# Weight conversion paced over the first expert, five pieces of it in the attention stage; token gather ahead of later weight loads; load queue in the attention plan

## The chip, the cores and the metric

The kernel runs on one core of a Trainium2 chip. The metric is the device time of one execution in microseconds (us). The engines are named as the profile names them: PE is TensorE (PEld its weight loads), DVE VectorE, ACT ScalarE, POOL GpSimd, SP SyncE, which here only issues DMAs.

## The reference

Three stages follow one another: a gated linear attention, a mixture of 8 experts with 384 tokens each, and a gated feed-forward layer that is the same for all tokens.

```python
def reference(**kwargs):
    attn_out = _attn_ref(q, k, v, a_re, a_im)      # (4, 8, 768, 48)
    x = attn_out.transpose(0, 2, 1, 3).reshape(B * S, H * D)   # 3072 x 384
    x = _moe_ref(x, w_gate, w1, w2)     # 8 experts, 384 -> 1024 -> 384
    return _moe2_ref(x, w_a, w_b, w_out)

def _attn_ref(...):          # complex decay a_re + i a_im, state 48 x 48 per head
    for t in range(S):
        new_re = ar * S_re - ai * S_im
        new_im = ar * S_im + ai * S_re
        S_re, S_im = new_re + outer(k[t], v[t]), new_im
        y[t] = q[t] @ S_re

def _moe_ref(x, w_gate, w1, w2):
    order = np.argsort(-(x @ w_gate).flatten())    # greedy: best logit first,
    # a token to one expert, an expert takes at most 384
    h = np.maximum(x[mask] @ w1[e], 0.0)
    out[mask] = h @ w2[e]

def _moe2_ref(x, w_a, w_b, w_out):      # 384 -> 1536 -> 384, float64 weights
    return ((x @ w_a) * (x @ w_b)) @ w_out
```

The weights of the last layer arrive in 64-bit floats and are handed to the kernel as pairs of 32-bit words.

## The kernel before, in words

**Attention.** The sequence is cut into 6 chunks of 128 steps; a pass i works on one chunk of two batches, 12 passes in all (`NB`). Each pass turns the decays into logarithms and angles (`gates`), sums them along the chunk on PE (`sums`), makes the turned q and k (`turned`), and for chunks after the first brings the state forward (`factor`, on 16 partitions). `unit` does the matmuls of one batch: transposes, scores, outer products, output. Nothing of this is issued directly: every step is a task of a `Plan`, with an engine, a planned duration, what it reads and writes, and a due time (`PERIOD` per pass). `Plan.order` walks through the tasks on a model of the engines and issues, each time, the ready task of lowest rank; the rank comes from the due time times `STRETCH`, the length of the chain behind the task, and an offset per kind of task from the table `EARLIER`; `SWITCH` is added where ACT would have to load another function table. SP's DMAs are tasks too (line 329 loads the decays, 332 and 334 q, k and v, 448 and 363 single rows for `factor`, 517 and 518 a swap of two halves of the state).

**Routing.** `route` finds each expert's threshold by five rounds of counting on DVE and PE, `lists` turns the choice into row numbers `idx`, `gather` fetches the 384 rows from `x_dram` with three indirect DMAs (tile `xg`, line 1216), transposes them on PE and splits them into two fp32r halves, `xh` and `xl`. The splits of weights and activations into such halves are helpers on lines 1153 (ACT) and 1154 (DVE). `w1_load` (line 1188) and `w2_load` (line 1202) fetch expert weights by indirect DMA, all from POOL. `R.keep` lets PE do matmuls whose result nobody reads.

**Experts.** `ffn(ph)` runs one expert: stage 1 (w1 and w2, 8 steps f with two `yield`s each, 144 matmuls of 128x384 on lines 1249 to 1251), then stage 2 (the last layer for the same tokens, 12 steps f with three `yield`s, 324 matmuls, lines 1301 and 1249 to 1251). The second-stage weights stay on chip in four `groups` of 9 pieces, 36 in all.

**Conversion.** `Glu.convert` makes these 36 pieces from the 64-bit words: a DMA of 384 KB (`load`, SP line 726), three steps on ACT (735, 741, 752) and three on DVE (745 `sign`, 749 `join`, 756 `low`). It is a generator with three `yield`s a piece, so 108 steps.

**What goes beside what.** During routing `beside` takes one conversion step for each routing step. In the first expert the loop at the end takes `CONV_RATE` = 4 conversion steps per `yield` of `ffn(0)`, and `SIDE_RATE` = 0.9 steps of the next expert's routing and loading (`later`), which may not load before the conversion has ended (`S["conv"]`):

```python
for n, _ in enumerate(ffn(ph)):
    due += CONV_RATE if ph == 0 else 0
    while due >= 1:
        due -= 1
        step(more, CONV_AFTER)
    k += SIDE_RATE if n < 16 else SIDE_RATE2
    while k >= 1:
        k -= 1
        step(it)
```

DVE takes its instructions in the order in which the code is written there (`manual_schedule`); the order of the other engines' instructions in this part is made by the compiler layer.

Of the kernel before, what the change touches and what calls it, by code (L numbers as in the profile page):

```python
# [10 lines left out]
F32 = mybir.dt.float32  # L11
# [23 lines left out]
SWITCH = 61.0  # L35
# [5 lines left out]
PIECES = 0  # L41
EARLIER = {'Acc': -2, 'Ae': 99, 'Aea': 39, 'Afw': 11, 'Ag': -75, 'Aln': -20, 'Apb': -27, 'AqkT': 9, 'Arec': 15, 'As2': -5, 'Asf': -11, 'Ath': 58, 'Axo': 8, 'AyT': -36, 'G-': -59, 'GW': -21, 'Gconsts': 2, 'Gmasks': 51, 'Gzeros': -28, 'PF': -33, 'PHH': -2, 'PLL': -39, 'PO': 68, 'PS': -40, 'PTT': 90, 'PX': 59, 'PY': 126, 'Sends': 69, 'Sfw': 67, 'Sim': -99, 'Sqk': 72, 'Sraw': -57, 'Sre': 2, 'Ssw': -147, 'Sv': -41, 'V-': 19, 'VAb': -10, 'VS': 99, 'Ve': 29, 'Vearly': -29, 'Veb': 55, 'Vft': -4, 'Vg': -28, 'Vlg': 5, 'Vn4': -38, 'Vnat': -69, 'Vr': 33, 'Vrho': 89, 'Vrt0': -55, 'Vrt1': -13, 'Vsetup': -54, 'Vxs': -152}
STRETCH = 3.699071
LONG = ("LL", "HH")
ENGINES = "PVASG"
SLOW = 1.03
SINGLE = 1
PATIENCE = 7
ENOUGH = 21.5
# [7 lines left out]
class Plan:  # L57
# [8 lines left out]
    def add(self, eng, dur, fn, reads=(), writes=(), due=0.0, take=None, drop=None, table=None, land=0.0):  # L66
        t = dict(n=len(self.tasks), eng=eng, dur=dur * SLOW if eng == "P" else dur, fn=fn, due=due, take=take, drop=drop, table=table, land=land,
# [21 lines left out]
    def order(self):  # L89
# [12 lines left out]
        free = dict.fromkeys(ENGINES, 0.0)  # L102
        for t in T:
            if not left[t["n"]]:
                waiting[t["eng"]].append(t["n"])
# [14 lines left out]
        while any(waiting.values()):  # L120
# [71 lines left out]
def attention(tc, q, k, v, a_re, a_im, wg, x_dram, consts, L, guard, router, glu, late):  # L192
# [8 lines left out]
    with ExitStack() as st:  # L201
# [26 lines left out]
        for nm, x in (("one", 1.0), ("shift", LIFT), ("tiny", LN(2.0e-6)), ("quarter", HALF_PI)):  # L228
            bias[nm] = cst.tile([128, 1], F32, name="b_" + nm)
            V.memset(bias[nm], x)  # L230
# [86 lines left out]
        def gates(i, due):  # L317
# [5 lines left out]
            load, land = (2.3, 2.2) if i < 2 else (0.6, 3.8)  # L323
            for us in parts(i):
# [3 lines left out]
                for nm, t, src in (("re", ld_re, a_re), ("im", ld_im, a_im)):  # L328
                    plan.add("S", took(load, us), lambda t=t, src=src, r=r, at=at, d2=d2: SP.dma_start(t[j][:, r], flat(src, at, d2)),
                             writes=[(nm, j, u) for u in us], due=due - 20 - 40 * (i < 2), land=land)  # L330
            for x, src in ((0, q), (1, k)):
                plan.add("S", load, lambda x=x, src=src: SP.dma_start(ld_qk[j][:, x], flat(src, base, dims)),
                         writes=[("qk", j, x)], due=due - 10, land=land)
            plan.add("S", load, lambda: SP.dma_start(vb[j].rearrange("p u h d -> p (u h) d")[:, :, 0:D], flat(v, base, dims)),
                     writes=[("v", j)], due=due - 4, land=land)
# [79 lines left out]
        def turned(i, due):  # L415
# [37 lines left out]
            if c < NCK - 1:  # L453
                w = (i + 2) % 4
                row(fw[w][:, 0], ("fw", w, 0), s2, both(ks2), 127)
                row(fw[w][:, 1], ("fw", w, 1), sn, both(ksn), 127)
            if c:
                w = i % 4
                row(fw[w][:, 2], ("fw", w, 2), s2, both(ks2), 0)
                row(fw[w][:, 3], ("fw", w, 3), sn, both(ksn), 0)  # L460

        def factor(i, due):
# [8 lines left out]
            plan.add("A", 0.22, lambda: A.activation(f[:, 4], f[:, 7], AF.Sin, bias=bias["quarter"][0:16]),  # L471
                     [kf[7]], [kf[4]], table="T", **a)
            plan.add("A", 0.22, lambda: A.activation(f[:, 5], f[:, 7], AF.Sin), [kf[7]], [kf[5]], table="T", **a)
            sh = [2 * H, 2, 2, D]

            def one():
                V.tensor_scalar(f[:, 0:3:2], f[:, 0:3:2], -1.0, 1.0, op0=OP.mult, op1=OP.add)
                V.tensor_tensor(w[:, 0:4].rearrange("p (a b) d -> p a b d", a=2), f[:, None, 0:2].to_broadcast(sh),
                                f[:, 2:4, None].to_broadcast(sh), op=OP.mult)
                V.tensor_tensor(w[:, 4], w[:, 0], w[:, 3], op=OP.add)  # L480
                V.tensor_tensor(w[:, 5], w[:, 1], w[:, 2], op=OP.subtract)
            plan.add("V", 0.92, one, kf[0:4], [kw, kf[0], kf[2]], **a)

            def two():
                V.tensor_tensor(w[:, 0:4].rearrange("p (a b) d -> p a b d", a=2), w[:, None, 4:6].to_broadcast(sh),
                                f[:, 4:6, None].to_broadcast(sh), op=OP.mult)
                V.tensor_tensor(w[:, 6], w[:, 0], w[:, 3], op=OP.subtract)
                V.tensor_tensor(w[:, 7], w[:, 1], w[:, 2], op=OP.add)
            plan.add("V", 0.66, two, [kw] + kf[4:6], [kw], **a)

            def three():
                V.scalar_tensor_tensor(w[:, 4], ends[:, i - 2, 0], math.exp(-2 * LIFT), ends[:, i, 1], op0=OP.mult, op1=OP.mult)
                V.tensor_tensor(w[:, 5], w[:, 4], f[:, 6], op=OP.mult)
                sh2 = [2 * H, 2, D]
                V.tensor_tensor(w[:, 8:10], w[:, 6, None].to_broadcast(sh2), w[:, 5, None].to_broadcast(sh2), op=OP.mult)
                V.tensor_tensor(w[:, 10], w[:, 7], w[:, 5], op=OP.mult)
# [1162 lines left out]
```

## Time and profile before

| | |
|---|---|
| median of 3 runs | 1066.19 us (1063.6 to 1066.37) |
| profiled execution, own time | 1064.48 us |
| its span, first to last instruction | 1062.9 us |
| mean granted TensorE clock | 0.975 of full |
| PE busy in the span | 994.7 us (94%) |
| DVE busy | 640.8 us (60%) |
| ACT busy | 501.8 us (47%) |

The shares are means over stages with different limits. Attention runs to about 288 us, routing to 329, the first expert from 329.1 to 436.6, and the seven others from there to the end. A busy PE is a modelled quantity, since matmuls overlap. [...]

### The profile page before, as it was taken

The page shows a single profiled execution, that of the slowest core. Times are in us where ns is not written, and L with a number is a line of the kernel's source. Part 1 is how long each engine was busy: PE and PEld are TensorE (multiplying, and loading weights), DVE is VectorE, ACT ScalarE, POOL GpSimd, SP SyncE. Part 2 cuts the span into 40 slices and gives each one's busy share as a digit, 9 for nine tenths or more (in the row PEclk, how much of TensorE's full clock was granted, in tenths as well). Part 3 has the DMA queues.
Part 4 walks back from the last instruction along what each step waited for, and adds up shares of the span by engine and source line. Part 5 has one row for each costly group of instructions (what it writes and reads, how often), then busy time and mean ns, then how long its engine had stood idle before and what let it go on. Part 6 is the DMA issues. An engine that isn't in the chain of part 4 may idle for free. (4 is left out here: it accounts for less than half of the span.)

```text
span 1062.9 us, 17395 instructions
## 1 busy us (share of the span) xinstructions
PE 994.7 (94%) x6660; PEld 901.2 (85%) x6660; DVE 640.8 (60%) x1596; ACT 501.8 (47%) x906; POOL 164.6 (15%) x217
## 2 busy tenths in 40 slices
PE   3899999999987699999999999999999999999994
PEld 1588787888746599999989999999999999999994
DVE  4689888998677987555366355455536644333321
ACT  6799898887426773332332332243233234233221
POOL 6000000000021003203112120320311213102001
PEclk9999999999968789999999999999999999999998
DMA  9866777344145644102112110310211212201000
GB/s 170 129 120 124 121 130 135 74 89 111 42 140 166 177 143 127 53 8 96 33 38 79 42 45 1 105 52 8 90 35 42 69 47 78 76 15 45 1 2 26
DMA packets 146764, 81.90 MB, mean 77 GB/s; under 512 B 130416, under 2 KB 132336, under 8 KB 146672
## 3 DMA queue, kind: packets, MB, share of 16 engines
q1 hardware_dynamic: 134448, 41.36, 20.4%
q0 software_dynamic: 12224, 39.34, 11.6%
q8 instruction: 54, 0.88, 0.3%
q14 instruction: 38, 0.31, 0.1%
HBM read 68.04 MB, written 9.44 MB: 73 GB/s over the span
## 5 line engine op out<-in xcount | busy, mean ns | idle before, releaser
L1301 PE MATMUL mm<-yh,glu 128*128 128x384 f32 x1152 | 241.7, 344 | 0.0
L1301 PEld LDWEIGHTS mm<-yh,glu 128*128 128x128 f32 x1152 | 201.5, 189 | 2.1 <-ACT yh L1153 0.4
L1335 DVE TENSOR_TENSOR g<-mm,a_s 128x384 f32<-128x384 f32 x96 | 53.4, 556 | 154.7 <-PE mm L1301 130.4
L1301 PE MATMUL mm<-yl,glu 128*128 128x384 f32 x576 | 133.2, 338 | 0.0
L1153 ACT ACTIVATE gh<-g 128x384 fp32r<-128x384 f32 x96 | 50.4, 525 | 163.5 <-DVE g L1335 163.5
L1330 ACT ACTIVATE a_s<-mm 128x384 f32<-128x384 f32 x96 | 47.1, 491 | 151.1 <-PE mm L1301 142.7
L1301 PEld LDWEIGHTS mm<-yl,glu 128*128 128x128 f32 x576 | 103.4, 187 | 0.0
L1249 PE MATMUL acc<-glu,gh 128*128 128x384 f32 x288 | 98.4, 342 | 0.0
L1250 PE MATMUL acc<-glu,gh 128*128 128x384 f32 x288 | 96.9, 336 | 0.0
L1251 PE MATMUL acc<-glu,gl 128*128 128x384 f32 x288 | 96.7, 337 | 0.1
L1202 POOL DMA_INDIRECT raw<-moe_w_in,i x64 | 64.2, 1004 | 171.0 <-DVE w2l L1154 121.5
L1154 DVE TENSOR_TENSOR gl<-g,gh 128x384 fp32r<-128x384 f32 x96 | 53.6, 558 | 40.8 <-ACT gh L1153 39.9
L1250 PE MATMUL acc<-hl,w2h 128*128 128x384 f32 x192 | 67.0, 349 | 5.2 <-DVE hl L1276 5.2
L1249 PE MATMUL mm<-xh,w1h 128*128 128x384 f32 x192 | 67.4, 352 | 0.4 <-ACT w1h L1153 0.3
L1251 PE MATMUL acc<-hh,w2l 128*128 128x384 f32 x192 | 66.1, 344 | 0.0
L1251 PE MATMUL mm<-xh,w1l 128*128 128x384 f32 x192 | 65.1, 339 | 1.1 <-DVE w1l L1154 1.1
L1249 PE MATMUL acc<-hh,w2h 128*128 128x384 f32 x192 | 65.8, 353 | 0.2 <-ACT hh L1275 0.2
L1250 PE MATMUL mm<-xl,w1h 128*128 128x384 f32 x192 | 65.0, 339 | 0.0
L1188 POOL DMA_INDIRECT raw<-moe_w_in,i x24 | 24.2, 1008 | 253.1 <-DVE left L1062 172.5
L1153 ACT ACTIVATE w1h<-raw 128x384 fp32r<-128x384 f32 x64 | 32.7, 521 | 54.1 <-PE mm L1250 51.6
L552 PE MATMUL bank<-qkT 96*128 96x128 f32 x384 | 54.1, 286 | 3.7 <-ACT qkT L543 3.4
L1154 DVE TENSOR_TENSOR w1l<-raw,w1h 128x384 fp32r<-128x384 f32 x64 | 34.9, 552 | 36.3 <-ACT w1h L1153 29.8
(277 smaller groups left out, 2007.7 us busy)
## 6 DMA issues: line engine op xcount, KB each, us to landing
stage<-moe_w_a_in SPq DMA_DIRECT2D x13, 384.0 KB, 3.2
vb<-v_in SPq DMA_DIRECT2D x12, 384.0 KB, 5.0
ld_qk<-q_in SPq DMA_DIRECT2D x12, 384.0 KB, 4.3
ld_qk<-k_in SPq DMA_DIRECT2D x12, 384.0 KB, 5.8
x_rows<-xo POOLq DMA_DIRECT2D x24, 192.0 KB, 2.4
stage<-moe_w_b_in SPq DMA_DIRECT2D x12, 384.0 KB, 3.2
stage<-moe_w_out_in SPq DMA_DIRECT2D x12, 384.0 KB, 3.5
ld_im<-a_im_in SPq DMA_DIRECT2D x11, 384.0 KB, 5.9
```

The source lines that it names most:

```text
L552: PE.matmul(p[:, x], qt[0:96, 4 * h4 + x, 1], qt[0:96, 4 * h4 + x, 0], start=True, stop=True)
L1153: a = A.activation(hi, src, AF.Copy)
L1154: return a, V.tensor_tensor(lo_, src, hi, op=OP.subtract)
L1188: G.indirect_dma_start(out=raw[:, j], out_offset=None, in_=w1r, in_offset=bass.IndirectOffsetOnAxis(ap=i1[:, j:j + 1], axis=0))
L1202: G.indirect_dma_start(out=raw, out_offset=None, in_=w2r, in_offset=bass.IndirectOffsetOnAxis(ap=i2[:, f:f + 1], axis=0))
L1249: PE.matmul(p, lh, rh, start=first, stop=False)
L1250: PE.matmul(p, lh, rl, start=False, stop=False)
L1251: PE.matmul(p, ll, rh, start=False, stop=last)
L1301: PE.matmul(p, a[:, j, c], b[:, j], start=(n == 0), stop=(n == 8))
L1330: A.activation(a_s, pa, AF.Copy)
L1335: V.tensor_tensor(g, pb, a_s, op=OP.mult)
```

## The change

Six things change. (1) Five pieces are converted inside attention, as tasks of the plan (`PIECES` 0 to 5). (2) The rest is paced: 1.2 steps per `yield` in stage 1 of the first expert, 2.2 in stage 2, and `Glu.need` takes the steps at once that a group is about to need; the steps of the next expert's routing go at 0.5 and then 1.15, and no longer wait for the conversion's end. (3) The first expert's w1 is fetched in two halves, and POOL, now in written order too, issues the gather behind the first half and one w2 load, and the other half behind the gather. (4) The dummy matmuls before the gather go from 24 to 36. (5) The plan counts the time that a DMA holds the load queue (`wire`), and its constants and the table `EARLIER`, one line of offsets for some fifty kinds, have new values. (6) `factor` takes the difference of angles first, so that one row r is sent by DMA in place of the rows of s2 and sn, and 10 small DVE instructions stand for 12.

```diff
-SWITCH = 61.0
+SWITCH = 186
...
-PIECES = 0
+PIECES = 5
...
-STRETCH = 3.699071
+STRETCH = 3.100414
...
-ENOUGH = 21.5
+ENOUGH = 21.0
...
+            sent = end
+            if e == "S":
+                sent = max(end, wire)
+                wire = sent + t["wire"]
             for u in users[n]:
                 left[u] -= 1
-                ready_at[u] = max(ready_at[u], end + t["land"] + (HOP[e] if T[u]["eng"] != e else 0.06))
+                ready_at[u] = max(ready_at[u], sent + t["land"] + (HOP[e] if T[u]["eng"] != e else 0.06))
...
-                row(fw[w][:, 0], ("fw", w, 0), s2, both(ks2), 127)
-                row(fw[w][:, 1], ("fw", w, 1), sn, both(ksn), 127)
+                row(fw[w][:, 0], ("fw", w, 0), r, both(kr), 127)
...
+            def angle():
+
+                V.scalar_tensor_tensor(f[:, 0], f[:, 7], 0.5 / PI, f[:, 0], op0=OP.mult, op1=OP.add)
+                V.tensor_tensor(f[:, 0], f[:, 0], f[:, 1], op=OP.subtract)
...
-WARM = 24
+WARM = 36
...
-CONV_RATE = 4
+SIDE_RATE0 = 0.5
+SIDE_RATE1 = 1.15
+CONV_RATE = 1.2
+CONV_RATE2 = 2.2
...
+    def need(self, pieces):
+
+        while self.at < min(pieces, 36) and next(self.more, 0) is None:
+            pass
...
+            else:
+                w1_half(0)
+
+        def w1_half(x):
             for j in range(3):
-                G.indirect_dma_start(out=raw[:, j], out_offset=None, in_=w1r,
-                                     in_offset=bass.IndirectOffsetOnAxis(ap=i1[:, j:j + 1], axis=0))
+                G.indirect_dma_start(out=S["raw1", 0][:, j, F1 // 2 * x:F1 // 2 * (x + 1)], out_offset=None, in_=w1s,
+                                     in_offset=bass.IndirectOffsetOnAxis(ap=S["i1", 0][:, 3 * x + j:3 * x + j + 1], axis=0))
...
             if ph == 0:
-                for f in (1, 2):
-                    w2_load(ph, f)
+                w2_load(ph, 1)
+                w1_half(1)
+                w2_load(ph, 2)
...
             for f in range(12):
+                glu.need(9 * (f // 3) + 3)
...
+                glu.need(9 * (f // 3) + 6)
...
-        with tc.manual_schedule(engines={V.engine}):
-            more = rest()
+        with tc.manual_schedule(engines={V.engine, G.engine}):
+            more = glu.more = rest()
...
-                    while S["moe"] < n - 1 or not S["conv"]:
+                    while S["moe"] < n - 1:
...
-            due = 0
+            due = glu.steps
             for n, _ in enumerate(ffn(ph)):
-                due += CONV_RATE if ph == 0 else 0
-                while due >= 1:
-                    due -= 1
+                due += CONV_RATE if n < 16 else CONV_RATE2
+                while glu.steps < min(due, 108):
                     step(more, CONV_AFTER)
-                k += SIDE_RATE if n < 16 else SIDE_RATE2
+                if ph == 0:
+                    k += SIDE_RATE0 if n < 16 else SIDE_RATE1
+                else:
+                    k += SIDE_RATE if n < 16 else SIDE_RATE2
```

**DVE in stage 1 of the first expert,** from the fifth `hl` (the second half of an activated block, which PE needs for the next step) to the sixth. `stage` and `glu` are conversion steps, `w1l` and `w2l` weight splits, the small names the next expert's routing. Before:

```order
L1276 SCALAR_TENSOR_TENSOR hl<-mm,hh 128x384
L756 TENSOR_TENSOR glu_2652<-stage,glu_2652 128x384
L749 SCALAR_TENSOR_TENSOR stage<-stage 128x384
L1154 TENSOR_TENSOR w1l<-raw_2949,w1h 128x384
L745 SCALAR_TENSOR_TENSOR stage<-stage 128x384
L1005 TENSOR_REDUCE cn<-misc 32x8
L756 TENSOR_TENSOR glu_2652<-stage,glu_2652 128x384
L749 SCALAR_TENSOR_TENSOR stage<-stage 128x384
L1007 TENSOR_TENSOR c_3323<-cn,rem 32x8
L1154 TENSOR_TENSOR w2l<-raw_3278,w2h 128x384
L745 SCALAR_TENSOR_TENSOR stage<-stage 128x384
L1276 SCALAR_TENSOR_TENSOR hl<-mm,hh 128x384
```

Changed, between the same two:

```order
L1307 SCALAR_TENSOR_TENSOR hl<-mm,hh 128x384
L1023 TENSOR_TENSOR c_3206<-cn,rem 32x8
L1170 TENSOR_TENSOR w1l<-raw_2944,w1h 128x384
L758 SCALAR_TENSOR_TENSOR stage<-stage 128x384
L1170 TENSOR_TENSOR w2l<-raw_3243,w2h 128x384
L754 SCALAR_TENSOR_TENSOR stage<-stage 128x384
L1029 TENSOR_REDUCE n<-misc 128x1
L1170 TENSOR_TENSOR w1l<-raw_2944,w1h 128x384
L765 TENSOR_TENSOR glu_2645<-stage,glu_2645 128x384
L1030 SCALAR_TENSOR_TENSOR lo<-n,steps,lo 128x1
L1307 SCALAR_TENSOR_TENSOR hl<-mm,hh 128x384
```

Six conversion steps stood between these two `hl`, now three. Over the stage, from the first `hl` to the first `yl`, 47 stood there before and 18 now; ahead of the first `hl` there were 25 and are 41; behind the first `yl` 36 and now 49.

**ACT just before the first expert,** where `raw_2953` and `raw_2948` are its w2 block 0, `raw_3028` and `raw_3035` its block 1, and `xh` the gathered rows behind their transposes. Before:

```order
L1153 ACTIVATE w1h<-raw_2949 128x384 x2
L1153 ACTIVATE w2h<-raw_2953 128x384
L1153 ACTIVATE w2h<-raw_3028 128x384
L741 ACTIVATE stage<-stage 128x384
L752 ACTIVATE glu_2247<-stage 128x384
L1153 ACTIVATE xh<-mm 128x3x128
```

Changed:

```order
L1169 ACTIVATE w2h<-raw_2948 128x384
L744 ACTIVATE stage<-stage 128x384
L750 ACTIVATE stage<-stage 128x384
L761 ACTIVATE glu_2645<-stage 128x384
L744 ACTIVATE stage<-stage 128x384
L750 ACTIVATE stage<-stage 128x384
L761 ACTIVATE glu_2645<-stage 128x384
L1169 ACTIVATE w2h<-raw_3035 128x384
L1169 ACTIVATE xh<-mm 128x3x128 x2
L744 ACTIVATE stage<-stage 128x384
L1169 ACTIVATE xh<-mm 128x3x128
```

The split of block 1 stands ahead of `xh` in both; the load of block 1 was issued by POOL ahead of the gather and is now issued behind it.

**SP at the start of the program.** Before, the imaginary parts come first:

```order
L329 DMA ld_im_124<-a_im_in 128x8x48 x2
L329 DMA ld_im_125<-a_im_in 128x16x48
L329 DMA ld_re_122<-a_re_in 128x8x48 x2
L329 DMA ld_re_123<-a_re_in 128x16x48
L334 DMA vb_172<-v_in 128x16x48
```

Changed:

```order
L334 DMA ld_re_122<-a_re_in 128x8x48 x2
L334 DMA ld_re_123<-a_re_in 128x16x48
L334 DMA ld_im_124<-a_im_in 128x8x48
L334 DMA ld_re_122<-a_re_in 128x16x48
L334 DMA ld_im_124<-a_im_in 128x8x48
L334 DMA ld_im_125<-a_im_in 128x16x48
```

The real parts of the first two passes now go first, and a real part of the third pass stands between the two halves of the first imaginary part.

## Rows read from the trace of the kernel before

**Rows 1.** The page: busy time of the engines, then PE and its granted clock in 40 slices.

```profile
PE 994.7 (94%) x6660; PEld 901.2 (85%) x6660; DVE 640.8 (60%) x1596; ACT 501.8 (47%) x906; POOL 164.6 (15%) x217
...
PE   3899999999987699999999999999999999999994
...
PEclk9999999999968789999999999999999999999998
```

**Rows 2.** Busy time by stage: stretch and length (us), PE, PEld, DVE, ACT, POOL, granted clock, DMA.

```profile
26.00:260.00 234.00, 219.95 (x1901) 181.03 (x1900) 197.28 (x375) 200.93 (x294) 10.34 (x19) 0.99 0.64 115
255.00:288.00 33.00, 31.15 (x341) 28.58 (x339) 24.36 (x59) 21.31 (x31) 2.70 (x5) 1.00 0.22 55
288.00:329.10 41.10, 31.74 (x249) 17.62 (x250) 28.89 (x94) 13.76 (x30) 11.75 (x12) 0.71 0.47 155
329.10:373.80 44.70, 34.17 (x170) 29.02 (x169) 41.26 (x113) 31.78 (x69) 3.01 (x3) 0.84 0.55 157
373.80:436.60 62.80, 62.09 (x366) 58.95 (x365) 46.84 (x135) 32.79 (x71) 12.11 (x11) 0.97 0.39 118
436.60:465.30 28.70, 28.70 (x178) 26.55 (x177) 17.20 (x43) 10.46 (x23) 5.93 (x6) 1.00 0.13 43
524.00:611.00 87.00, 87.00 (x532) 82.31 (x531) 46.94 (x136) 27.03 (x56) 16.81 (x17) 1.00 0.16 51
```

**Rows 3.** What PE waited for, 340 to 380 us: us in total, times, longest.

```profile
PE acc L1250 <- DVE hl L1276: 5.2, 5, 1.9
```

**Rows 4.** Groups of DVE instructions, 330 to 436 us: count, then busy us and mean ns.

```profile
L756 DVE TENSOR_TENSOR glu<-stage,glu 128x384 fp32r<-128x384 f32 x29 | 16.0, 553 | 1.0 <-ACT glu L752 0.8
L749 DVE SCALAR_TENSOR_TENSOR stage<-stage 128x384 int32<-128x384 int32 x29 | 16.0, 552 | 0.3 <-ACT glu L752 0.2
L745 DVE SCALAR_TENSOR_TENSOR stage<-stage 128x384 int32<-128x384 int32 x28 | 15.5, 554 | 3.8 <-ACT stage L735 3.7
```

**Rows 5.** Timeline of DVE in stage 1 of the first expert: start, duration.

```profile
349.02 0.55 DVE L745 SCALAR_TENSOR_TENSOR stage<-stage 128x384 int32<-128x384 int32 x1
349.49 0.55 DVE L1154 TENSOR_TENSOR w1l<-raw,w1h 128x384 fp32r<-128x384 f32 x1
```

**Rows 6.** Timeline of the start: first ACT, DVE and PE work on the decays.

```profile
8.18 0.52 ACT L345 ACTIVATE ln<-ld_re 128x384 f32<-128x384 f32 x1 [5.95 <-DMA ld_re<-a_re_in]
...
9.39 0.56 DVE L352 TENSOR_TENSOR rho<-ld_im,rec 128x384 f32<-128x384 f32 x1 [6.38 <-ACT rec L345]
...
15.56 1.62 PE L375 MATMUL pair<-e,Ws 128*128 128x384 f32 x2 [15.56 <-DVE e L348]
```

**Rows 7.** Timeline of the last pass: first row by DMA, first and last instruction of the factor.

```profile
269.30 0.52 SPq L448 DMA_DIRECT2D fw<-sn  x1
...
272.82 0.19 DVE L477 TENSOR_SCALAR fw<-fw 16x96 f32<-16x96 f32 x1
...
275.14 0.19 DVE L497 SCALAR_TENSOR_TENSOR ft<-ft 16x48 f32<-16x48 f32 x1
```

**Rows 8.** Timeline of POOL's indirect DMAs before the first expert.

```profile
315.06 1.11 POOL L1202 DMA_INDIRECT raw<-moe_w_in,i  x1 [0.30 <-issue]
316.48 0.95 POOL L1216 DMA_INDIRECT xg<-x_rows,idx  x1 [0.30 <-issue]
...
318.98 0.95 POOL L1216 DMA_INDIRECT xg<-x_rows,idx  x1 [0.30 <-issue]
```

**Rows 9.** Timeline of PE there: dummy matmuls, first transposes, first matmul of the expert.

```profile
314.32 4.07 PE L888 MATMUL mm<-offs,ones 128*128 128x384 bf16 x24
323.61 0.87 PE L1229 MATMUL mm<-ident,xg 128*128 128x128 f32 x3 [5.21 <-DMA raw<-moe_w_in,i]
...
329.14 0.96 PE L1249 MATMUL mm<-xh,w1h 128*128 128x384 f32 x2
```

**Rows 10.** Tile raw (expert weights), 300 to 345 us: issue to landing.

```profile
DMA to landing us min/median/max: 3.1/5.2/8.4
```

**Rows 11.** What PE waited for in attention, 0 to 288 us.

```profile
PE pair L375 <- DVE n L391: 7.3, 6, 2.2
```

More of the change, by code (lines that the diff above doesn't have):

```diff
@@ L227, in attention @@
         bias = {}
-        for nm, x in (("one", 1.0), ("shift", LIFT), ("tiny", LN(2.0e-6)), ("quarter", HALF_PI)):
+        for nm, x in (("one", 1.0), ("shift", LIFT), ("tiny", LN(2.0e-6))):
             bias[nm] = cst.tile([128, 1], F32, name="b_" + nm)
@@ L322, in gates @@
             a = dict(due=due)
-            load, land = (2.3, 2.2) if i < 2 else (0.6, 3.8)
+            load, land, wire = (2.3, 2.2, 0.0) if i < 2 else (0.6, 3.8, 2.0)
             for us in parts(i):
@@ L470, in factor @@
                      [kf[6]], [kf[6]], table="E", **a)
[L471 to L489, printed above, removed]
@@ L498, in factor @@
-            plan.add("V", 0.9, three, [kw, kf[6], ("ends", i - 2, 0), ("ends", i, 1)], [kw], **a)
+            sh = [2 * H, 2, D]
+            def angle():
+                V.scalar_tensor_tensor(f[:, 0], f[:, 7], 0.5 / PI, f[:, 0], op0=OP.mult, op1=OP.add)
+                V.tensor_tensor(f[:, 0], f[:, 0], f[:, 1], op=OP.subtract)
+                V.tensor_scalar(f[:, 1], f[:, 0], TURN, TURN, op0=OP.add, op1=OP.subtract)
+                V.tensor_tensor(f[:, 0], f[:, 0], f[:, 1], op=OP.subtract)
@@ new lines, in factor, with size @@
+            plan.add("V", 0.86, angle, [kf[0], kf[1], kf[7]], [kf[0], kf[1]], **a)
+            plan.add("A", 0.22, lambda: A.activation(f[:, 3], f[:, 0], AF.Sin, scale=PI), [kf[0]], [kf[3]], table="T", **a)
+            plan.add("A", 0.22, lambda: A.activation(f[:, 2], f[:, 0], AF.Sin, scale=2 * PI), [kf[0]], [kf[2]], table="T", **a)
+            def size():
+                V.scalar_tensor_tensor(w[:, 4], ends[:, i - 2, 0], -math.exp(-2 * LIFT), ends[:, i, 1], op0=OP.mult, op1=OP.mult)
+                V.tensor_tensor(w[:, 5], w[:, 4], f[:, 6], op=OP.mult)
@@ L499, in factor @@
+            plan.add("V", 0.85, three, [kw, kf[2], kf[3]], [kw, kf[3]], **a)
             kp = ("F", i)
@@ L627, in attention @@
             kr, kw = ("raw", x % 2), ("word", x % 2)
-            plan.add("S", 0.6, (lambda x=x: glu.load(x)) if x else weights, [], [kr] + (taken if x == 0 else []), land=2.5, **end)
+            plan.add("S", 0.6, (lambda x=x: glu.load(x)) if x else weights, [], [kr] + (taken if x == 0 else []), land=2.5, wire=1.2, **end)
             if x == 0:
@@ L700, in __init__ @@
         self.src = [w.bitcast(I32) for w in (wa, wb, wo)]
-        self.stage, self.groups, self.at = stage, [], 0
+        self.stage, self.groups, self.at, self.steps = stage, [], 0, 0
+        self.more = iter(())
+    def need(self, pieces):
+        while self.at < min(pieces, 36) and next(self.more, 0) is None:
+            pass
     def place(self, pool, to):
@@ L760, in convert @@
         i0 = self.at
+        self.steps = 3 * i0
         if i0 == 0:
@@ L768, in convert @@
                 self.low(i - 1)
+                self.at = i
+                self.steps += 1
                 yield
@@ L771, in convert @@
             self.bits(i + 1)
+            self.steps += 1
             yield
@@ L776, in convert @@
             self.high(i)
+            self.steps += 1
             yield
         self.low(35)
+        self.at = 36
+        self.steps += 1
         yield
@@ L1175, in weights @@
             yield
-            V.tensor_tensor(i1, f1, R.wi1, op=OP.add)
+            if ph:
+                V.tensor_tensor(i1, f1, R.wi1, op=OP.add)
+            else:
+                i1 = rk.tile([128, 6], I32, name="i1h", bufs=1)
+                V.tensor_tensor(f1, f1, R.wi1, op=OP.add)
+                for x in range(2):
+                    V.tensor_scalar(i1[:, 3 * x:3 * x + 3], f1, 2.0, float(x), op0=OP.mult, op1=OP.add)
             yield
@@ L1307, in last @@
                 gh, gl = gs[f]
+                glu.need(9 * (f // 3) + 9)
                 for i in range(3):
```

41 lines of the change are left out of this document (22 added, 19 removed).

## The prediction

> **What bounds the kernel now.** The page first: PE is busy for 994.7 of 1062.9 us and DVE for 640.8, so PE looks like the bound everywhere. The slices contradict that in one place: from about a quarter of the span to a little past a third, PE's digits fall and its granted clock with them [rows 1]. The table by stage says where [rows 2]. In an expert of the middle (524 to 611 us) PE is busy for all of 87.0 us at clock 1.00 and DVE for 46.9: PE-bound, with nothing to gain. In stage 1 of the first expert PE is busy for 34.2 of 44.7 us at clock 0.84, and DVE for 41.3, which is 92%. There DVE sets the pace. The waits agree: the wait that PE met most in 340 to 380 us is for `hl` on DVE, 5.2 us in five pieces [rows 3], and the low clock stretches the rest. The groups say what fills DVE: three conversion lines, 86 instructions of some 0.55 us [rows 4]. Stage 1 of the second expert, the same 144 matmuls and nine more without conversion beside them, takes 28.7 us [rows 2]. Stage 2 of the first expert takes 62.8 us with PE busy for 62.1. Attention (26 to 260 us) is nearly full on PE, 219.95 of 234.00, with DVE at 84% and ACT at 86%; routing and gather, 288 to 329.1 us, run at clock 0.71 [rows 2].
>
> **The change, part by part.** The sum is made against the profiled execution's own time, 1064.48 us (span 1062.9); the median of the runs shown is 1.7 us above it.
>
> *Price of a conversion step on DVE.* It shows 0.55 us, but in a full queue the next starts 0.47 us later (349.02, 349.49) [rows 5]. I count 0.47.
>
> *Stage 1.* By the order of instructions, 47 conversion steps stood in it and 18 do now: 29 x 0.47 = 13.6 us less on DVE. The next expert's routing goes from 14 steps to 8 (0.9 and 0.5 times 16); at about 0.5 us each, 3 us less. So DVE has 41.3 - 16.6 = 24.7 us of work. At the 92% that DVE reached when it was the bound that is 26.8 us, just under what PE needs: 28.7 us less nine matmuls of the expert before. At 87.0 us for 468 matmuls and the small ones, those nine are 1.6 us, so 27.1. PE becomes the bound, narrowly. I take 28.5 us, 1.4 above the floor, since the two queues are almost equally full: **-16.2 us**. Bounds: 27.1 (-17.6) and, if DVE's spread work still stops PE at each step, 32 (-12.7).
>
> *Stage 2.* It receives what stage 1 loses, apart from the pieces done earlier: 49 steps in place of 36, +6.1 us on DVE, and the six routing steps, +3: 46.8 + 9.1 = 56 us, at 92% 61 us. The floor is 87.0 - 28.7 = 58.3 us. DVE is therefore the bound over most of the stage, up to the last conversion step, and PE catches up behind it. I take 61.5: **-1.3 us**. Bounds 58.3 (-4.5) and 67 (+4).
>
> *Gather.* POOL issued two w2 blocks ahead of `xg`; the second, at 315.06, goes behind it, so the three gathers start 1.4 us earlier, with 768 KB of w1 ahead of them and not 1.5 MB [rows 8]. PE waited for them for 5.2 us, until 323.61 [rows 9]. With 36 dummy matmuls (12 more at 0.17) it is occupied until about 320.4, and the transposes that follow would no longer start behind that gap at half clock. But they don't set the start of the expert: on ACT and DVE the split of w2 block 1 stands ahead of `xh` and `xl`, and this block's load is now behind the gather, at about 318.8 us. It lands 3.1 to 5.2 us later (minimum and median of such loads) [rows 10]. With 3.1: landed at 321.9, split at 322.4, three `xh` and a conversion step at 0.5 each to 324.4, `xl` and first matmul at about 325.3, against 329.14 [rows 9]: -3.8. With 5.2: -1.7. The queue ahead is short, so I take 3.5: **-3.4 us**. [...]
>
> *Routing.* The same number of conversion steps stands in it; two small DVE instructions more and one w1 index in two halves: +0.3 us.
>
> *Attention's start.* SP used to load 768 KB of imaginary parts ahead of the first real part, which ACT met at 8.18 us; the first product with an imaginary part followed at 9.39 and PE began at 15.56 [rows 6]. Now 768 KB of real parts stand ahead of the first imaginary one. It lands when the real part did, and ACT's two steps (9.39 - 8.18 = 1.2 us) are done by then: **-1.2 us**. Bounds: the second half of the imaginary part waits for 384 KB more than the first, +1; or the first half's chain runs unhindered by others, -3.6.
>
> *Attention's middle and tail.* The five pieces put 15 steps on ACT (7.8 us at 0.52) and 15 on DVE (7.1). By the order they stand in the last two passes. Between 255 and 288 us DVE idles for 8.6 us and ACT for 11.7 [rows 2]: they fit if they go into the gaps. `factor` loses two of twelve instructions that took 2.5 us (272.82 to 275.33) [rows 7], 0.4 us ten times over; and its row r can leave ahead of the sines, where the rows of s2 and sn left at 269.30, behind them, in the pass whose end is the end of attention. In front of that stand conversion steps of 0.5 us. I take -1.0 us for the tail and nothing for the re-ordered middle: the same matmuls stand there, and no row says whether the new order has fewer gaps. Bounds: half of the 14.05 us that PE idles in 26 to 260 us, -7, or as much more, +7.
>
> Sum: -16.2 - 1.3 - 3.4 + 0.3 - 1.2 - 1.0 = -22.8; 1064.5 - 22.8 = 1041.7, **1042 us**.
>
> **The rivals.**
>
> *The clock stays low.* PE's granted clock was 0.84 in the stage where DVE kept stopping it and 0.97 and 1.00 where it didn't [rows 2]. If DVE's 56 us in stage 2 come as many short stops, stage 2 could run at 0.84: 58.3 / 0.84 = 69.4, 8 us above my 61.5, and stage 1 27.1 / 0.84 = 32.3, +3.8: 1054 us. For it: DVE has no slack there. Against: with PE busy for 62.1 of 62.8 us before, the clock was 0.97. [...]
>
> *Attention pays for the pieces.* If the 15 steps don't fall into gaps but ahead of the tail's own work, 7.8 us of ACT lie on the path, also because the 384 KB loads stand in SP's queue ahead of the last swaps: 1042 + 8 = 1050. For it: ACT at 86% and the tail is a chain. Against: idle time in 255 to 288 us.
>
> *Attention gains.* The new order takes half of PE's idle time: 1035.
>
> *Slower.* The re-planned order loses the pace of attention: a wait like that for n on DVE (2.2 us at its longest [rows 11]) in every one of 12 passes. It decides from 22.8 / 12 = 1.9 us a pass; at 2.5 us it is +30 us, 1072. Against: six such waits made 7.3 us in all, and the plan still orders by readiness.
>
> *The pacing doesn't arrive.* `need` or the recorded order pulls the steps forward again, and the time is 1064. The order of instructions speaks against it.
>
> **How the numbers follow.** My forecast 0.50; the clock 0.13; attention pays 0.17; attention gains 0.13; slower 0.03, and 0.01 for a mishap of the same sign; no pacing 0.03. The forecast's own bounds are 1035 to 1049 (stages and gather added where they can meet). The range reaches to the rivals on both sides and leaves out the far ones: 1034 to 1053. 0.3% is 3.2 us, about what a measurement of this kernel can tell from no change: faster 0.93, within 0.03, slower 0.04.
>
> **What would show it.** Right: stage 1 near 28 us with PE's clock at 1.00; conversion lines of DVE among stage 2; PE's gap before the transposes under 2 us, and the next wait there for the split of w2 block 1, not for the gather; attention ending within a few us of 288; the other experts unchanged at 87. Wrong: waits for `hl`, `gl` or `yl` of more than 5 us in stage 2, a clock under 0.9 there, or attention ending past 294.

## The result, and the profile after

The changed kernel takes 1039.33 us (median of 4 runs, 1038.54 to 1041.0) against 1064.89 us for the kernel before (1062.88 to 1066.37): ratio 0.9763, 95% interval 0.9739 to 0.9787. The forecast was 1042, the range 1034 to 1053. The total was met; of its larger terms only stage 1 was, as the profile shows. The profiled execution took 1038.54 us, span 1036.9. Its page, with the rows that answer to [rows 1]:

```profile
PE 977.9 (94%) x6672; PEld 895.0 (86%) x6672; DVE 633.5 (61%) x1577; ACT 500.0 (48%) x906; POOL 168.4 (16%) x220
...
PE   2899999999869989999999999999999999999994
...
PEclk9999999999789999999999999999999999999997
```

The dip of PE and of its clock comes sooner and is shorter: two slices of the clock at 7 and 8 tenths of full speed, where four stood at 6 to 8. The table by stage (stretch and length, then PE, PEld, DVE, ACT, POOL, clock, DMA, GB/s) answers to [rows 2]:

```profile
26.00:240.00 214.00, 206.25 (x1902) 175.86 (x1901) 192.84 (x361) 197.66 (x291) 9.79 (x18) 1.00 0.65 123
...
267.70:310.70 43.00, 32.48 (x261) 17.73 (x261) 30.52 (x100) 15.57 (x33) 15.03 (x15) 0.73 0.50 155
310.70:338.50 27.80, 27.79 (x157) 26.54 (x158) 25.35 (x75) 18.33 (x40) 2.98 (x3) 0.92 0.39 115
338.50:406.40 67.90, 62.97 (x378) 57.93 (x377) 53.96 (x157) 39.48 (x84) 11.32 (x11) 1.00 0.45 134
406.40:435.10 28.70, 28.70 (x177) 26.56 (x177) 17.16 (x43) 10.46 (x23) 5.92 (x6) 1.00 0.13 43
495.00:582.00 87.00, 86.64 (x529) 81.97 (x528) 46.62 (x136) 26.92 (x56) 16.78 (x17) 1.00 0.15 51
```

Stage 1 is PE-bound now (27.8 us, PE busy for all of it); stage 2 is not (62.97 of 67.9). The largest difference stands ahead of both. The reduction on each `unit`'s output, 24 in all, from the changed kernel and then from the one before:

```profile
L602 DVE TENSOR_REDUCE L<-bank x24: 169/182/193, 55.0 to 267.1; 128x8 f32<-128x32 f32 x24
```

```profile
L602 DVE TENSOR_REDUCE L<-bank x24: 168/186/193, 57.7 to 287.3; 128x8 f32<-128x32 f32 x24
```

Attention ends 20.2 us sooner. Cut at the same events, the spans differ so:

| part | before | after | difference | forecast |
|---|---|---|---|---|
| start to the last output of attention | 287.3 | 267.1 | -20.2 | -2.2 |
| from there to `idx` of the first expert (routing) | 27.4 | 28.9 | +1.5 | +0.3 |
| `idx` to the first expert's first matmul | 14.4 | 14.7 | +0.3 | -3.4 |
| stage 1 | 44.7 | 27.8 | -16.9 | -16.2 |
| stage 2 | 62.8 | 67.9 | +5.1 | -1.3 |
| the rest, seven experts | 626.3 | 630.5 | +4.2 | 0 |
| sum | 1062.9 | 1036.9 | -26.0 | -22.8 |

### The profile page after: what moved, and what is told of

Its sections match the earlier page's. It is cut to its first block, busy times and chain, and to the rows that moved or that the text cites. A ratio compares the mean times of both kernels' runs of the same rounds, so it can differ in the third digit from the quotient of the medians.

```text
span 1036.9 us, 17318 instructions
## 1 busy us (share of the span) xinstructions
PE 977.9 (94%) x6672; PEld 895.0 (86%) x6672; DVE 633.5 (61%) x1577; ACT 500.0 (48%) x906; POOL 168.4 (16%) x220
## 4 chain that ended last, share of the span: by engine, by line
PE 84%; DVE 5%; DMA 3%; ACT 3%; issue 3%; POOL 1%; another core or an unknown queue 1%; SPq 0%; POOLq 0%; DVEq 0%; ACTq 0%
PE mm L1332 27%; PE acc L1280 8%; PE acc L1282 8%; PE acc L1281 8%; PE pair L380 5%; PE mm L1280 4%; PE bank L552 4%; PE pair L540 3%; PE mm L1282 3%; PE mm L1281 3%; PE bank L563 2%; PE bank L580 2%; PE bank L600 2%; PE bank L587 2%; DMA fw<-r 1%
## 5 line engine op out<-in xcount | busy, mean ns | idle before, releaser
L1233 POOL DMA_INDIRECT raw<-moe_w_in,i x64 | 63.8, 997 | 161.2 <-DVE w2l L1170 132.6
L1280 PE MATMUL acc<-hh,w2h 128*128 128x384 f32 x192 | 66.7, 349 | 0.0
L1281 PE MATMUL acc<-hl,w2h 128*128 128x384 f32 x192 | 64.4, 335 | 0.0
L1282 PE MATMUL acc<-hh,w2l 128*128 128x384 f32 x192 | 64.3, 335 | 0.0
L1212 POOL DMA_INDIRECT raw<-moe_w_in,i x21 | 21.2, 1011 | 222.8 <-DVE left L1078 172.3
L1280 PEld LDWEIGHTS acc<-glu,gh 128*128 128x128 f32 x288 | 54.2, 188 | 1.1 <-ACT gh L1169 0.9
```

Source lines behind the costliest of these rows:

```text
L1233: G.indirect_dma_start(out=raw, out_offset=None, in_=w2r, in_offset=bass.IndirectOffsetOnAxis(ap=i2[:, f:f + 1], axis=0))
L1280: PE.matmul(p, lh, rh, start=first, stop=False)
L1281: PE.matmul(p, lh, rl, start=False, stop=False)
L1282: PE.matmul(p, ll, rh, start=False, stop=last)
```

## The experiments

All of them compute the whole reference. Their results first. Each ratio is taken to runs of the kernel before that were made beside it (medians 1063.75 to 1066.36 us), so equal times can stand beside unequal ratios. The last four columns come from one profile each, good to 0.1 us, and both stages are cut there at the first recorded matmul that reads `yh`, about 1 us later than in the tables above.

| kernel | median us | ratio to before, interval | last output | `idx` to first matmul | stage 1 | stage 2 |
|---|---|---|---|---|---|---|
| before | 1064.89 | | 287.3 | 14.4 | 45.7 | 61.7 |
| changed | 1039.33 | 0.9763 (0.9739 to 0.9787) | 267.1 | 14.7 | 28.6 | 67.0 |
| after_again | 1035.57 | 0.9738 (0.9706 to 0.9770) | 265.9 | 10.8 | 28.8 | 67.0 |
| att_only | 1043.1 | 0.9802 (0.9786 to 0.9818) | 270.7 | 13.3 | 45.7 | 60.4 |
| factor_alone | 1084.54 | 1.0194 (1.0177 to 1.0211) | 317.8 | 11.0 | 27.5 | 72.0 |
| old_factor | 1072.7 | 1.0080 (1.0063 to 1.0097) | 312.9 | 11.6 | 27.1 | 66.7 |
| no_fit | 1118.81 | 1.0497 (1.0477 to 1.0517) | 348.3 | 13.1 | 28.8 | 66.5 |
| no_wire | 1101.84 | 1.0338 (1.0319 to 1.0357) | 329.8 | 15.5 | 28.6 | 67.0 |
| pieces0 | 1035.79 | 0.9737 (0.9720 to 0.9753) | 266.7 | 10.7 | 27.6 | 71.9 |
| p0_w2_first | 1039.99 | 0.9786 (0.9746 to 0.9827) | 266.6 | 11.1 | 28.4 | 72.4 |
| p0_pool_free | 1040.3 | 0.9790 (0.9751 to 0.9829) | 266.7 | 15.6 | 27.2 | 67.6 |
| p0_side_late | 1035.47 | 0.9736 (0.9705 to 0.9767) | 266.1 | 15.3 | 28.3 | 63.1 |
| after_side_late | 1035.47 | 0.9704 (0.9687 to 0.9720) | 270.8 | 14.1 | 29.1 | 64.3 |

### Attention: which part of the change carries it

**att_only.** The kernel before with the attention hunks of the diff (table, constants, `wire`, `factor`, pieces), without the later ones.

> The kernel before with the attention part of the change alone (new table of offsets and constants, load queue in the plan, new factor, five pieces); routing, gather and first expert as before. Theory (the attention part is worth 20 us by itself): attention's last steps end at 267 us, not 287; the first expert, with 15 of 108 conversion steps fewer to do, is 4 to 7 us shorter than before; 1065 - 20 - 6 = 1039, that is as fast as the whole change, and the pacing would be worth nothing on top. Rival (pacing is worth its 16 us of stage 1 whatever attention does): attention ends at 267, stage 1 of the first expert stays near 44 us, since DVE is still full there; 1065 - 20 = 1045 to 1047, and stage 2 ends up to 5 us sooner than in the changed kernel.

Measured: 1043.1 us, attention ends at 270.7, stage 1 takes 45.7, stage 2 60.4. The rival came nearer: fewer steps left don't unload stage 1, the pacing does. Stage 2 was 6.6 us shorter than in the changed kernel (up to 5 expected), and the total lies 2 us below the rival's range, although this profile began 3.8 us late (see the last section). The whole later part of the change is worth only 4 to 7 us on top (ratios 0.9802 against 0.9763 and 0.9738), not 16: what stage 1 gains is largely given back, below.

**factor_alone** and **old_factor.** The first has the new `factor` under the old table, the second the new table over the old `factor`.

```diff
 factor_alone, against the changed kernel
-PIECES = 5
+PIECES = 0
-SWITCH = 186
+SWITCH = 61.0
...
-                sent = max(end, wire)
 old_factor, against the changed kernel
-                row(fw[w][:, 0], ("fw", w, 0), r, both(kr), 127)
+                row(fw[w][:, 0], ("fw", w, 0), s2, both(ks2), 127)
+                row(fw[w][:, 1], ("fw", w, 1), sn, both(ksn), 127)
...
```

> The later part of the change (pacing, gather, dummy matmuls) with the new factor, but attention's old table and constants, no load queue in the plan and no pieces. Theory (the order made attention 20 us shorter): attention ends at 285 to 288 us, within 2 us of before. Rival (the shorter chain of factor, one row in place of two and ten DVE instructions in place of twelve, freed the passes): attention ends at 275 or sooner. Stage 1 27 to 29 us in both; stage 2 has to take the 15 steps that attention no longer does, 15 x 0.47 = 7 us on DVE, so 73 to 75 us if DVE bounds it, 68 if it doesn't. Total by the theory 1039 + 20 + 6 = 1065, that is no gain over the kernel before; by the rival 1050.

> The changed kernel with the factor of before (rows of s2 and sn, twelve DVE instructions, both behind the sines), all else as changed. If the order carries the 20 us: attention ends within 3 us of 267.7, total 1039 to 1043. If the shorter factor carries them: attention ends at 280 to 288, total 1052 to 1060. If the table only fits the tasks it was made for: in between, with new waits for the rows of fw on DVE.

Both simple theories fell. Attention ends at 317.8 and 312.9 us: either one without the other makes it 26 to 31 us *longer* than before, only the two together shorten it. From the first output to the 24th, an output comes every 9.22 us in the changed kernel and every 9.98 in the one before; with the halves mixed it is 11.2 and 11.1. What old_factor's DVE waits for, 60 to 240 us (total, times, longest), and its row for that stretch with the columns of the table by stage:

```profile
DVE Ab L559 <- PE bank L557: 9.7, 10, 2.3
DVE L L607 <- PE bank L605: 8.8, 6, 4.2
DVE eb L439 <- ACT ea L407: 3.7, 1, 3.7
...
60.00:240.00 180.00, 162.17 (x1387) 135.42 (x1389) 145.08 (x266) 147.56 (x214) 7.28 (x14) 0.93 0.53 107
```

The waits are spread over many names. My reading, which no run tests by itself, is that the orders of the engines no longer fit one another. The clock adds to it: granted were 0.93 here and 0.95 in factor_alone, where the kernel before has 0.99 and the changed one 1.00, which is up to 13 of the 180 us (an estimate, 7% of the stretch). A table fitted anew to the old factor was not tried, so these runs don't show that the gain needs the new factor.

**no_fit** and **no_wire.** One line each of the changed kernel:

```diff
-EARLIER = {'Acc': -166, 'Ae': -70, ...}
+EARLIER = {}
...
-                sent = max(end, wire)
+                sent = max(end, 0.0)
```

> The changed kernel with an empty table of offsets (all zero), so that the plan orders attention by due times and chains alone; same tasks, same other constants. If the 20 us come from a table that was fitted to just these tasks, attention loses its pace: 24 outputs at 11 us each in place of 9.2, as with the two mixed kernels, attention ends at 300 to 320 us, total 1070 to 1090. If they come from the tasks (shorter factor, load queue in the plan), most of the pace stays without a table: attention ends at 265 to 280 us.

> The changed kernel whose plan doesn't count how long a transfer holds the load queue; the table and all other constants as changed. If counting the queue is what makes the plan's times true and the order good: waits for loads and for the swapped state (Sb, 8.3 us in the kernel before) come back on DVE and attention ends 10 us later or more. If the table's fit is all: attention is slower by the same amount, but spread over all waits, with none for loads standing out. If the queue hardly changes the order: within 3 us of 267.

Without a table attention ends at 348.3 us, 81 us later, and later than expected: an output comes every 13.3 us (granted clock 0.85 from 60 to 240 us). Without the load queue in the plan it ends at 329.8 (clock 0.93), and here one wait stands out, on DVE, 60 to 240 us, where the changed kernel has 5.0 us:

```profile
DVE fw L479 <- DMA fw<-r: 28.4, 7, 6.8
```

SP's queue in the same profile, ahead of one of them (start, duration):

```profile
107.52 0.54 SPq L337 DMA_DIRECT2D ld_qk<-q_in  x1
108.11 1.94 SPq L337 DMA_DIRECT2D ld_qk<-k_in  x1
110.13 2.34 SPq L453 DMA_DIRECT2D fw<-r  x2
```

```profile
114.22 0.20 DVE L479 TENSOR_TENSOR fw<-fw 16x48 f32<-16x48 f32 x1 [4.02 <-DMA fw<-r]
```

A load of k took 1.94 us of SP's queue, the rows (3.0 KB each) were issued behind it, at 110.13 us, and DVE, at the instruction that reads them, stood for 4.02 us. The plan without `wire` had put DVE there as if the rows left at once. This shows one way in which the counted queue matters. The wait for the swapped state, also expected, did not come back (0.8 us in all). A third of the loss lies ahead of the first output, which comes at 76.8 us in place of 55.0; from there an output comes every 11.0 us:

```profile
L602 DVE TENSOR_REDUCE L<-bank x24: 168/181/192, 76.8 to 329.8; 128x8 f32<-128x32 f32 x24
```

How much of the 63 us between 267.1 and 329.8 is owed to the queue alone, and how much to a table fitted with it, this run doesn't separate.

**pieces0.** `PIECES` back at 0, all else as changed.

> The changed kernel with no conversion pieces in attention (all 36 later). If the pieces lay in gaps of ACT and DVE, attention ends at 266 to 268 us as with them, and stage 2 of the first expert takes 15 x 0.47 = 7 us more (75 us): 1046. If they cost attention their time on ACT (15 x 0.52 = 7.8 us), attention ends at 260, and the two cancel: 1039. A third outcome, an offsets table that fits one set of tasks alone, would show as an attention that ends later than 270 without the pieces.

Attention ends at 266.7, as with the pieces: they lay in gaps. Stage 2 took 71.9, 4.9 more than 67.0 (7 expected), but not by DVE's price of the steps alone: PE idled 2.4 us more, and the clock, 1.00 in the changed kernel's stage 2, was 0.95 in this one. The 1046 expected for this case did not come. The total, 1035.79 (0.9737), can't be told from the two measurements of the changed kernel (0.9763, 0.9738): the pieces are worth nothing that was measured.

### Stage 2, the gather, and the experts behind

**after_again.** The changed kernel once more.

> The changed kernel once more, nothing altered. In its first profile ACT stood still for 3.1 us before the third xh (307.0 to 310.2 us) and PE started the first expert at 310.7 at half clock, 14.7 us after idx; the kernel without pieces, with the same code there, took 10.7 us. If the stop belongs to this kernel: idx to first matmul 14 to 15 us again, and the experts behind spaced by 89.5 us. If it belongs to that one execution: 10.7 to 11.7 us and 89.1 us, and this profile ends some 5 us sooner than the first one. Time 1037 to 1041 by the first, 1034 to 1037 by the second.

The second answer: 10.8 us and 89.1 us, 1035.57. The stop in the first profile, on ACT (start, duration, then the idle time and what ended it):

```profile
304.36 0.52 ACT L1169 ACTIVATE w2h<-raw 128x384 fp32r<-128x384 f32 x1 [1.49 <-DMA raw<-moe_w_in,i]
304.79 0.47 ACT L1169 ACTIVATE xh<-mm 128x384 fp32r<-128x384 f32 x1
305.88 0.49 ACT L1169 ACTIVATE xh<-mm 128x384 fp32r<-128x384 f32 x1 [0.62 <-PE mm L904]
306.49 0.55 ACT L744 ACTIVATE stage<-stage 128x384 int32<-128x384 uint32 x1
310.17 0.49 ACT L1169 ACTIVATE xh<-mm 128x384 fp32r<-128x384 f32 x1 [3.12 <-remote]
```

belongs to executions, not to the kernel. The second profile has no such row. By the order of instructions this xh waits for PE alone, whose transposes are on record until 304.57. The trace also holds the times of the signals between engines: PE's signal for these transposes came at 310.14, 5.6 us behind their recorded end and 0.02 us ahead of xh, whereas in the kernel before the three such signals come 0.01 us behind the recorded ends (the last at 328.33 us). So ACT did wait for PE; why PE signalled so late stays open. PE had no work on record for the last 5.49 us before the expert; the granted clock is 0.50 from 310.7 to 314 us, which makes the 0.92 of stage 1 above.

**p0_pool_free** and **p0_w2_first**, on the kernel without pieces. The first hands POOL's order back to the compiler layer, which moves the gather behind four loads; the second moves one load ahead of the gather.

```diff
-        with tc.manual_schedule(engines={V.engine, G.engine}):
+        with tc.manual_schedule(engines={V.engine}):
...
-            for f in range(3 if ph else 1):
+            for f in range(3 if ph else 2):
                 w2_load(ph, f)
...
-                w2_load(ph, 1)
                 w1_half(1)
```

> The kernel without pieces, with POOL's order left to the compiler layer again. By the order of instructions this moves one thing: the three gathers for the first expert go behind w2 block 1 and the second half of w1, four DMA issues of 1.25 us, so 5 us later. If the early gather is worth what that says: the transposes start 4 to 5 us later, the first expert 14.5 to 16 us after idx, and the total is 1039 to 1041. If something else sets the start (the dummy matmuls and the split of w2): under 2 us. The experts behind keep 89.1 us in both, as POOL's order there is the same.

> The kernel without pieces, with the load of w2 block 1 ahead of the token gather again and the rest behind it. If the split of w2 block 1 sets the start of the first expert (the reason given in the prediction): the split comes 1.3 us sooner, the gathers 1.3 us later, and the first matmul stays within 0.5 us of 10.7 us after idx or comes sooner. If the gather sets it: the transposes start 1.3 us later and the first matmul is 1.0 to 1.5 us later, 11.7 to 12.2 us after idx. Total 1036 to 1037 either way, under what 3 rounds can tell, so it is read from the profile.

The late gather costs what was expected: the first matmul comes 15.6 us after `idx`, not 10.7, and the median is 1040.3 (pieces0: 1035.79; the intervals of the ratios just touch). The transposes then wait for it on PE of p0_pool_free, where the granted clock is 0.50 from 304 to 312 us. That the first wait is for the gather is my reading: the profile names one of SP's queues, and in the kernel before this transpose waits for 13 semaphores (322.97 to 323.57 us).

```profile
305.59 0.87 PE L1261 MATMUL mm<-ident,xg 128*128 128x128 f32 x3 [2.63 <-DMA stage<-moe_w_out_in]
309.03 0.80 PE L1261 MATMUL mm<-ident,xg 128*128 128x128 f32 x3 [0.93 <-issue]
```

In pieces0 they follow the dummy matmuls without a gap and take 0.49 us, as in the changed kernel at a granted clock of 1.00 (300 to 304.6 us):

```profile
300.81 0.98 PE L904 MATMUL mm<-offs,ones 128*128 128x384 bf16 x5
301.62 0.49 PE L1261 MATMUL mm<-ident,xg 128*128 128x128 f32 x3
...
305.41 0.62 PE L1280 MATMUL mm<-xh,w1h 128*128 128x384 f32 x2 [0.69 <-ACT xh L1169]
```

In p0_pool_free's profile stage 2 was 4.3 us shorter than in that of pieces0 (67.6 against 71.9): PE idled 4.5 us in it, not 7.3, and its clock was at half for 3.4 us, not 6.8 (granted 0.95 over the stage of pieces0; six matmuls on `yh` take 2.27 us there at 388.66 and 1.22 at 395.38, and four take 1.65 at 385.87 in p0_pool_free). Why these two differ is open. p0_w2_first is inconclusive: 11.1 us with a stop of 1.2 us among them, between the two theories, and a median 3 us above what either gave, with a wide interval. The experts behind keep 89.1 us with either order of POOL, as expected.

**p0_side_late** and **after_side_late**, without and with the pieces: two steps more between the second expert's gather and the transposes of its rows.

```diff
-SIDE_RATE1 = 1.15
+SIDE_RATE1 = 1.2
...
                 w2_load(ph, 2)
+            if ph == 1:
+                yield
+                yield
             yield
```

> The kernel without pieces, with two more steps between the gather for the second expert and the transposes of its rows (steps taken at 1.2 in place of 1.15 a yield, so that they still fit). PE waited 4.2 us for xg there, in stage 2 of the first expert (71.9 us), and 0.4 us in the kernel before. If PE's wait for the gather is what stage 2 lost: stage 2 falls to 67 to 69 us and the total by 3 to 4 us, to 1032. If DVE's work bounds the stage (36 steps of conversion before, 64 here), the wait only moves to the next name and the stage stays at 71 to 73 us.

> The changed kernel (five pieces in attention) with two more steps between the second expert's gather and its transposes, at 1.2 steps a yield. Without the pieces this took stage 2 of the first expert from 71.9 to 63.1 us. If the wait of PE for the next expert's lists and gather is what the pacing lost, it holds with the pieces too: stage 2 60 to 63 us in place of 67.0, yh to yh of the first expert 91 to 92 us in place of 96.7, total 1030 to 1034. If the pieces had already freed that time: stage 2 stays at 66 to 68 us, total 1035 to 1040.

Stage 2 falls from 71.9 to 63.1 (67 to 69 expected) and, with the pieces, from 67.0 to 64.3 us (60 to 63 expected). PE's waits in stage 2 of pieces0, then of p0_side_late, each with the row of the stage:

```profile
333.00:405.00 72.00, 64.72 (x373) 59.51 (x373) 59.99 (x167) 44.66 (x98) 14.25 (x11) 0.95 0.49 150
...
PE mm L1261 <- DMA xg<-x_rows,idx: 4.2, 3, 2.1
PE misc L1140 <- DVE lt L1133: 1.2, 1, 1.2
PE misc L1129 <- DVE rhs L1125: 0.9, 1, 0.9
PE acc L1280 <- ACT gh L1169: 0.7, 1, 0.7
```

```profile
338.00:402.00 64.00, 61.10 (x368) 56.15 (x367) 57.72 (x156) 44.79 (x97) 12.41 (x10) 1.00 0.52 165
...
PE mm L1264 <- DMA xg<-x_rows,idx: 1.8, 1, 1.8
PE misc L1140 <- DVE lt L1133: 0.8, 1, 0.8
```

So stage 2 lost much of its time to waits for the next expert's gather and lists, during which PE did nothing else. Of the 8.8 us, 4.4 are PE's idle time (7.28 and 2.90) and some 3.4 the clock, which was at half for 6.8 us in pieces0 and not at all in p0_side_late. Of the 2.7 us with the pieces, at clock 1.00 in both, 2.2 are idle time. The lists (`rhs`, `lt`) come from DVE, where conversion steps stand directly ahead of them, so conversion is not cleared as a cause of those waits.

The gain did not reach the total as expected (1032, and 1030 to 1034). p0_side_late takes 1035.47, as pieces0 does with 1035.79; its profile lost 4.6 us ahead of the first matmul (15.3 and 10.7 us after `idx`). after_side_late has the lowest ratio of all, 0.9704, below the first measurement of the changed kernel (0.9763) with intervals apart, but the interval of the second (0.9706 to 0.9770) touches it. Its profile began with two of the delays that come and go (attention 3.8 us later, 14.1 us to the first matmul). It is faster than the kernel before beyond doubt, and than the changed one by 0 to 6 us.

## Why the prediction was right or wrong

**Stage 1 (-16.2): right**, -16.9. DVE was busy for 25.35 us (24.7 forecast), PE is the bound, and att_only shows that without the pacing the stage keeps its 45.7 us. The clock was 0.92 in it, not the 1.00 forecast, and 0.94 in after_again: in both the first matmuls of the stage take 0.52 us, where later ones take 0.33 to 0.34.

**Stage 2 (-1.3, at most +4): wrong**, +5.1. The step that failed is "DVE is therefore the bound over most of the stage". DVE was busy for 53.96 us, near the 56 forecast, but that is 79% of the stage, and none of the named waits (`hl`, `gl`, `yl`) came. PE waited instead for work of the second expert:

```profile
PE mm L1261 <- DMA xg<-x_rows,idx: 1.8, 3, 1.0
PE misc L1129 <- DVE rhs L1125: 1.5, 1, 1.5
PE misc L1140 <- DVE lt L1133: 1.0, 1, 1.0
```

I had priced the routing steps, raised from 0.9 to 1.15 a `yield`, as DVE time alone. The higher rate also shortens the distance between a gather and the transposes that need it, and PE took up nothing else while it waited for these: it idled 4.93 us in the stage, 0.71 before. after_side_late gave 2.7 us back, p0_side_late 8.8, of which some 3.4 were the clock. The rival "the clock stays low" did not come in the changed kernel (1.00 in stage 2 of both its profiles), but it is not out in general: without the pieces the clock in that stage was 0.95 (pieces0) and 0.91 (p0_w2_first, where six matmuls on `yh` take 2.27 us at 391.85 and 1.22 at 398.80).

**Gather (-3.4): right in size where nothing else intervened, +0.3 in the first profile.** With the early gather the first matmul comes 10.7 to 11.6 us after `idx` in four profiles (14.4 before: -3.7 to -2.8), and 13.1 to 15.5 in five. Four of these five show what the prediction named, ACT's split of w2 block 1 waiting for its load (1.49 us in the changed kernel, 2.43 in no_wire, against 0.17 in pieces0), but four of the five also PE's late signal, a stop of 1.9 to 4.3 us before a later `xh`. no_fit has the wait without the stop:

```profile
387.32 0.52 ACT L1169 ACTIVATE w2h<-raw 128x384 fp32r<-128x384 f32 x1 [3.22 <-DMA raw<-moe_w_in,i]
...
390.44 1.01 PE L1280 MATMUL mm<-xh,w1h 128*128 128x384 f32 x2 [4.47 <-issue]
```

From the start of this split to the first matmul it is 3.1 us here, and the same 3.1 us in pieces0 and after_again, where the split starts 2.4 and 2.3 us sooner after `idx`. These three fit the path of the forecast, with the split 3.2 to 5.4 us behind the issue of its load (3.1 to 5.2 forecast for the landing). The term failed where PE's late signal came on top, which no row before had.

**Attention (-1.2 and -1.0): wrong**, -20.2; this is the term that carried the result. The start was a size, -2.75 where -1.2 was forecast: PE began at 12.81 us, not 15.56; the first logarithm ran at 3.90 us in place of 8.18. The step that failed is "nothing for the re-ordered middle", with a bound of half of PE's idle time, 7 us. The 24 outputs took 17.5 us less from first to last, more than all of PE's idle time there, 9.5 us. So PE's busy time was no measure of what the order left. 60 to 240 us, before and after:

```profile
60.00:240.00 180.00, 173.57 (x1590) 146.24 (x1591) 157.99 (x298) 160.15 (x234) 8.66 (x16) 0.99 0.61 113
```

```profile
60.00:240.00 180.00, 176.85 (x1693) 153.99 (x1692) 165.99 (x317) 167.60 (x249) 8.63 (x16) 1.00 0.60 119
```

PE's busy time rises by 3.3 us, its recorded instructions by 103, 6%. Per output PE was busy for 0.964 x 9.98 = 9.62 us before and 0.983 x 9.22 = 9.06 now, for the same matmuls: of the 0.76 us that an output became cheaper, 0.56 came out of time that the profile calls busy (an estimated 0.1 of it is the clock, 0.99 and 1.00). The weight loads (PEld) say it better: 81% of the stretch before, 86% after. By an estimate from the 81% (the other 19% of 180 us) the bound on this term would have been -34 us; by idle time it was -7. The rival "attention gains" had the sign, at 0.13 and less than half the size; att_only shows that the attention part carries the gain by itself, and factor_alone, old_factor and no_fit that the order and the tasks it was fitted to carry it together. Why this order is faster than the old one was not traced further. One lead is on record, DVE's largest wait in that stretch before, for the swapped state, and the same wait after:

```profile
DVE Sb L521 <- DMA sw<-rtb: 8.3, 4, 2.8
```

```profile
DVE Sb L521 <- DMA sw<-rtb: 0.6, 1, 0.6
```

**Routing (+0.3)** measured +1.5; the other profiles have 27.7 to 30.3 us where this one has 28.9. **The experts behind (0)** measured +4.2, of which 2.1 stays in after_again (628.4 us): 89.1 us each in place of 88.9. POOL's written order is not the cause (89.1 us without it too); the cause is open.

So the total was met by compensation, against the forecast -18.0 in attention and -0.7 in stage 1, and +6.4, +3.7, +4.2 and +1.2 elsewhere. The 1042 was luck. Without attention the measured parts add up to -5.8 us, where -20.6 was forecast: still faster, but by a quarter of it.

## What to carry to other kernels

Where PE looks full, don't bound what a new order can give by PE's idle time; the share of weight loads was the better bound here (-34 us by the estimate above and -7 by idle time, with -17.5 measured from the first output to the last). A table of offsets belongs to the tasks and the model that it was fitted with. With the other factor or without the queue in the model, attention ended 31 us (factor_alone, from the kernel before), 46 and 63 us (old_factor and no_wire, from the changed kernel) later, on the same matmuls; the five conversion pieces, on the other hand, could be taken out at no cost to attention. When work for the next stage is spread faster over this one, check the distance between each transfer and its first reader on the engine that is the bound. And before a difference between two profiles is put down to an edit, look at the granted clock of the stage in both.

## What the runs showed of the hardware

The same PE instructions come to their shorter durations at different times in different executions. Eight transposes of attention's start, in the changed kernel and then in att_only:

```profile
37.92 1.08 PE L540 MATMUL pair<-ident,nat 128*96 128x128 f32 x8 [0.35 <-ACT ea L407]
```

```profile
39.44 1.94 PE L540 MATMUL pair<-ident,nat 128*96 128x128 f32 x8
...
46.92 1.04 PE L540 MATMUL pair<-ident,nat 128*96 128x128 f32 x8
```

PE's first matmul starts at 12.81 and 12.88 us in the two, and up to 35 us PE's starts agree within 0.1 us, in the same order. Then eight transposes take 1.08 us in one, and in the other 1.94 us at 39.44 and 42.49, and 1.04 only at 46.92. My reading is that this is PE's clock: the durations differ as they do elsewhere between a granted 0.50 and 1.00 (three transposes in 0.85 to 0.87 us at 323.6 to 328 us of the kernel before, in 0.49 at 302 to 304.6 us of the changed one). The clock column can't show it, as it has 1.00 from 12 us on in the changed kernel, whose matmuls shorten only at 35 us (0.53 us at 33.79, 0.32 at 35.45). The first output comes at 55.0 and 58.8 us, and at the end of attention the difference is 3.6 us (267.1 and 270.7). after_side_late has the later step too (1.94 us at 39.35, 1.04 at 46.93). Together with the stops before `xh` (1.9 to 4.3 us) this is nearly as large as the spread between executions of the changed kernel, 1031.8 to 1041.0 us, and as large as the effect of several of the edits. That the two make up this spread isn't shown, as only two of its executions have a profile.
